# The last row of W_down in thirteen transfers of 16, 15, 14 … 5 and 2 partitions

## The chip, the cores and the metric

The kernel runs on one core of a Trainium2 chip. A core has TensorE (PE, with weight loads shown apart as PEld), VectorE (DVE), ScalarE (ACT), GpSimd (POOL) and SyncE (SP), and 16 DMA engines that move data between HBM and the core's SBUF memory. SBUF has 128 partitions. The metric is device time in microseconds, the median of several executions. One execution is recorded by the hardware profiler; it gives the page, the trace and all the views quoted here.

## The reference

Two layers follow each other for four sequences of one token each (B = 4, D = 576). The first is attention over a window of the last 4096 positions of a cache; the second is a gated MLP with F = 4608:

```
W = min(4096, max(256, Sk // 4))                    # 4096 of Sk = 16384
q = (layernorm(x) @ wq) -> [4, 32 heads, 1, 128]
scores = q . k * 128**-0.5 ; p = softmax(scores) ; o = p . v     # 16 kv heads
h = x + o.reshape(4, 1, 4096) @ wo

gate = layernorm(h) @ W_gate                        # [4, 4608]
up   = layernorm(h) @ W_up
hh   = gate * (gate > 0) * up
out  = h + hh @ W_down                              # W_down is [4608, 576]
```

All inputs are bfloat16. The cache windows and the weights that must be read are 159.6 MB.

## The kernel before

The program of each engine is written out by hand, in order. A small class `Sched` counts: an operation names what it depends on, and the class turns that into a wait on a semaphore value (`op`, `dma`, `wait`, lines 50 to 100). A transfer adds 16 to its semaphore when all of it has landed. Transfers that have the same key share a semaphore, so a wait on the last of several waits for the sum of all of them.

All large loads stand in one list, `transfers`, and SP issues them in that order (`prog_sync`, line 265). They go into one SBUF tensor, `pool`, which has four slots of 4 MB. A transfer waits until the reader of what stood there before is done (its `free` list). The order is: wq in two pieces (lines 234 and 236), then for 16 groups of four heads the K and V cache windows, alternating (lines 238 to 242), then wo (243), W_gate and W_up in two pieces each (245 to 249), and last W_down (251 to 256). The cache is the bulk of it: 32 transfers of 4 MB.

While the cache streams in, DVE transposes K (line 402), PE forms scores and the products with V (helper `mm`, lines 460 to 471), ACT takes the exponentials and POOL the maximum over partitions. After the last V, PE multiplies with wo (the `ATTN` step, lines 547 to 553), DVE adds the residual and normalises, PE forms gate and up, ACT and DVE combine them into `hhT`, and PE multiplies with W_down (lines 585 to 594).

W_down goes into SBUF with 36 of its rows on each partition: row p * 36 + j is at partition p, place j. A "row" of the transfer list means one place j on all 128 partitions, 576 values or 1152 bytes on each. The six transfers of before take 14, 9, 6, 4, 2 and 1 of these places, each over all 128 partitions. They wait for `ATTN`, because the space they fill was that of wo. PE waits for each transfer in turn and then adds its rows to the two output tiles, two matmuls a row (320 and 256 columns). When the last row is in, ACT and DVE copy one part each to `out_sb` (OUT0, line 367, and OUT1, line 454), and SP writes it out (line 268).

The x input is loaded by ACT's own queue at the start (line 303), over 4 partitions; the output is stored in the same shape.

Of the kernel before, what the change touches and what calls it, by code (L numbers as in the profile page):

```python
# [13 lines left out]
D = 576  # L14
# [24 lines left out]
JJ = 36  # L39
# [63 lines left out]
def bass_sequential_preLN__sliding_block_cached__glu_gated_reglu__decode_kernel(  # L103
# [12 lines left out]
    with ExitStack() as es:  # L116
        cnt = [0]

        def sb(name, shape, dt):
            return es.enter_context(nc.sbuf_tensor(name, shape, dt))  # L120

        pool = sb("pool", [128, NSLOT * QUAD], BF16)
# [77 lines left out]
        transfers = []  # L200
# [49 lines left out]

        wd_sb = pool[:, 0:FC * D].rearrange("p (j n) -> p j n", j=JJ)
        WD = [(0, 14), (14, 23), (23, 29), (29, 33), (33, 35), (35, 36)]
        for k, (f0, f1) in enumerate(WD):
            transfers.append((("wd", k), f"wd{k}", ["ATTN"],
                              lambda e, f0=f0, f1=f1: e.dma_start(
                                  out=pool[:, f0 * D:f1 * D], in_=B_W_down.rearrange("(p j) n -> p (j n)", j=JJ)[:, f0 * D:f1 * D])))

        def feat(c):
            return slice(c, c + 509, 4) if c < 4 else slice(512, D)
# [1 line left out]
        def land(name):  # L261
            return ("L",) + (name if isinstance(name, tuple) else (name,))
# [194 lines left out]
        def prog_pe(S):  # L457
# [126 lines left out]

            for k, (f0, f1) in enumerate(WD):
                deps = [land(("wd", k))]
# [44 lines left out]
```

## Time and profile before

| | |
|---|---|
| median of 3 runs | 377.74 us (377.72 to 378.39) |
| the profiled execution | 378.37 us |
| its span in the trace | 377.0 us |
| granted TensorE clock, mean | 0.923 |
| PE busy | 291.9 us (77%) |
| DVE busy | 222.5 us (59%) |
| HBM read | 159.58 MB, 423 GB/s over the span |
| transfers of W_down issued by SP | 353.51 to 356.21 us |

The span is the time from the first to the last instruction in the trace; the time of an execution has a little more around it. In the views, `out<-in` names the tiles an instruction writes and reads, "SPq" is SP's issuing of transfers, and the number after L is the line in the kernel. The busy share of DMA is a mean over the 16 engines. Below the page, the trace keeps one record for each DMA packet (its queue, start, duration and size, but not the engine that moved it) and the time of each semaphore update of a transfer.

### The profile page before, as it was taken

How to read it: one execution, taken by the hardware profiler on the slowest of the kernel's cores; microseconds unless marked ns; L12 is line 12 of the kernel's file. 1: busy time of each engine (PE TensorE's matmuls, PEld its weight loads, DVE VectorE, ACT ScalarE, POOL GpSimd, SP SyncE). 2: the span in 40 equal slices, each digit the busy share in tenths (PEclk: the TensorE clock that was granted, in tenths of full speed). 3: DMA queues.
4: the chain of work that ended last, by engine and by line, in shares of the span. 5: the costliest groups of instructions: out<-in, count | busy, mean ns of one | idle time of the engine just before them, and what ended most of it. 6: DMA issues, size and time to landing. Idle time of an engine off the chain costs nothing.

```text
span 377.0 us, 2565 instructions
## 1 busy us (share of the span) xinstructions
PE 291.9 (77%) x1384; PEld 67.9 (18%) x740; DVE 222.5 (59%) x169; ACT 53.1 (14%) x138; POOL 12.1 (3%) x34
## 2 busy tenths in 40 slices
PE   1408299969996999499939996799689967977675
PEld 0001012212221222022202221122112211222213
DVE  3037577696859494859476856775676658221230
ACT  3003402010220012001200220021002010101020
POOL 6000000000000000000000000000000000000000
PEclk9999879998998799989998998999869995996989
DMA  8999999999999999999999999999999999999995
GB/s 334 431 445 441 403 438 440 441 418 424 437 441 428 414 441 436 435 410 441 441 426 421 435 445 428 431 422 441 431 435 415 441 435 428 447 428 416 418 417 245
DMA packets 6507, 159.74 MB, mean 424 GB/s; under 512 B 729, under 2 KB 865, under 8 KB 1633
## 3 DMA queue, kind: packets, MB, share of 16 engines
q1 hardware_dynamic: 6488, 159.59, 98.7%
q8 instruction: 8, 0.13, 0.1%
q14 instruction: 3, 0.02, 0.0%
q10 hardware_dynamic: 8, 0.00, 0.0%
HBM read 159.58 MB, written 0.00 MB: 423 GB/s over the span
## 4 chain that ended last, share of the span: by engine, by line
DMA 53%; DVE 28%; PE 15%; ACT 2%; issue 1%; SPq 1%; POOL 0%; DVEq 0%
DMA pool<-in_A_k_cache_dram 48%; DVE kT L402 19%; PE sc L464 5%; PE sc L466 5%; DMA pool<-in_B_W_down_dram 5%; DVE acc L421 4%; DVE own_sb L418 2%; PE val L464 2%; PE val L466 2%; DVE probT L415 1%; DVE rmx L405 1%; ACT P L347 1%; DVE o_bf L440 0%; ACT L347 0%; ACT qz L336 0%
## 5 line engine op out<-in xcount | busy, mean ns | idle before, releaser
L402 DVE STREAM_TRANSPOSE kT<-pool 128x2048 f32<-128x2048 f32 x64 | 142.9, 2279 | 34.9 <-DMA pool<-in_A_k_cache_dram 33.9
L464 PE MATMUL sc<-kT,qz 128*128 128x512 bf16 x240 | 104.4, 435 | 28.7 <-DVE kT L402 28.7
L466 PE MATMUL sc<-kT,qz 128*128 128x512 bf16 x256 | 110.4, 431 | 18.3 <-DVE kT L402 16.2
L464 PE MATMUL val<-pool,probT 128*64 128x512 bf16 (+2 forms) x328 | 102.4, 360 | 4.6 <-DMA pool<-in_B_W_down_dram 4.6
L466 PE MATMUL val<-pool,probT 128*64 128x512 bf16 x256 | 96.2, 379 | 0.0
L464 PEld LDWEIGHTS sc<-kT,qz 128*128 128x128 bf16 x256 | 26.9, 105 | 154.8 <-issue 76.3
L464 PEld LDWEIGHTS val<-pool,probT 128*64 128x64 bf16 (+1 forms) x328 | 31.4, 104 | 88.0 <-issue 78.1
L405 DVE TENSOR_REDUCE rmx<-sc 128x1 f32<-128x1024 f32 x16 | 19.6, 1225 | 42.4 <-PE sc L466 42.4
L342 ACT ACTIVATE pmax<-mask,rmx 128x8 f32<-128x8 f32 x16 | 4.8, 301 | 241.3 <-DVE rmx L405 241.3
L415 DVE STREAM_TRANSPOSE probT<-P 128x1024 bf16<-128x1024 bf16 x16 | 19.9, 1245 | 20.7 <-ACT P L347 20.7
L347 ACT ACTIVATE P<-sc,bias 128x1024 bf16<-128x1024 f32 x16 | 17.8, 1113 | 13.3 <-DVE bias L410 13.3
L336 ACT COPY qz<-qrep 32x128 bf16<-32x128 bf16 x64 | 18.8, 294 | 0.6
L294 POOL PARTITION_ALL_REDUCE bcm<-pmax x16 | 5.9, 367 | 312.8 <-ACT pmax L342 312.8
L421 DVE TENSOR_REDUCE acc<-own_sb 128x128 f32<-128x1024 f32 x8 | 15.2, 1895 | 0.3
L418 DVE TENSOR_TENSOR own_sb<-val,mask 128x1024 f32<-128x1024 f32 x8 | 9.5, 1193 | 8.3 <-PE val L466 8.3
L464 PE MATMUL sc<-pool,oX 128*4 128x288 bf16 x32 | 10.2, 345 | 0.4 <-ACT oX L356 0.4
L408 DVE SCALAR_TENSOR_TENSOR t<-bcm,mask 128x8 f32<-128x8 f32 x16 | 2.7, 167 | 13.3 <-POOL bcm L294 13.3
L466 PE MATMUL sc<-pool,oX 128*4 128x288 bf16 x32 | 10.2, 343 | 0.0
L464 PE MATMUL sc<-qT,sel 32*128 32x128 bf16 x4 | 0.3, 284 | 9.8 <-DVE qT L428 9.8
L443 DVE TENSOR_TENSOR h_row<-sc,x_bf 4x576 f32<-4x576 f32 x1 | 0.7, 745 | 11.9 <-PE sc L466 11.9
L464 PE MATMUL sc<-col,foe 4*128 4x512 bf16 x16 | 6.4, 399 | 0.7 <-ACT qrep L322 0.7
L464 PE MATMUL val<-pool,xnT 128*32 128x512 bf16 x16 | 2.6, 628 | 5.0 <-DMA pool<-in_A_wq_dram 5.0
(98 smaller groups left out, 74.4 us busy)
## 6 DMA issues: line engine op xcount, KB each, us to landing
pool<-in_A_k_cache_dram SPq DMA_DIRECT2D x16, 4096.0 KB, 26.9
pool<-in_A_v_cache_dram SPq DMA_DIRECT2D x16, 4096.0 KB, 26.8
pool<-in_A_wo_dram SPq DMA_DIRECT2D x1, 4608.0 KB, 18.3
pool<-in_B_W_gate_dram SPq DMA_DIRECT2D x1, 4608.0 KB, 17.8
pool<-in_B_W_up_dram SPq DMA_DIRECT2D x1, 4608.0 KB, 24.0
pool<-in_A_wq_dram SPq DMA_DIRECT2D x1, 4096.0 KB, 13.6
pool<-in_B_W_down_dram SPq DMA_DIRECT2D x1, 2016.0 KB, 13.7
pool<-in_B_W_down_dram SPq DMA_DIRECT2D x1, 1296.0 KB, 16.4
```

The source lines that it names most:

```text
L294: S.op(g, lambda e, i=i: e.partition_all_reduce(bcm[:, i % 2, :], pmax[:, i % 2, :], 128, bass_isa.ReduceOp.max), deps=deps, name=("PAR", i))
L336: S.op(a, lambda e, src=src, dst=dst: e.copy(out=dst, in_=src), deps=deps, name=("QZ", i) if g == 3 else None, signal=g == 3)
L342: S.op(a, lambda e, i=i: e.activation(out=pmax[:, i % 2, :], in_=mask[:, 1, :], func=ACT.Identity, bias=rmx[:, i % 2:i % 2 + 1], scale=1.0 ...
L347: S.op(a, lambda e, i=i: e.activation(out=Pb[:, (i % 2) * 1024:(i % 2 + 1) * 1024], in_=sc[:, (i % 2) * 1024:(i % 2 + 1) * 1024], func=ACT ...
L402: S.op(v, lambda e: e.transpose(out=dst, in_=src), deps=deps, name=("TR", f))
L405: S.op(v, lambda e: e.tensor_reduce(out=rmx[:, i % 2:i % 2 + 1], in_=sc[:, (i % 2) * 1024:(i % 2 + 1) * 1024], axis=AX.X, op=ALU.max), dep ...
L408: S.op(v, lambda e: e.scalar_tensor_tensor(out=t8[:, :], in0=bcm[:, i % 2, :], scalar=-SCALE, in1=mask[:, 0, :], op0=ALU.mult, op1=ALU.mul ...
L415: S.op(v, lambda e: e.transpose(out=pT[i % NPT], in_=Pb[:, (i % 2) * 1024:(i % 2 + 1) * 1024]), deps=[("EXP", i)] + ([("PV", i - NPT)] if ...
L418: S.op(v, lambda e: e.tensor_tensor(out=own_sb[:, :].rearrange("p (x d) -> p x d", d=DH), in0=val[:, :].rearrange("p (x d) -> p x d", d=DH ...
L421: S.op(v, lambda e: e.tensor_reduce(out=acc[:, w % 2, :], in_=own_sb[:, :].rearrange("p (x d) -> p d x", d=DH), axis=AX.X, op=ALU.add), de ...
L464: return e.matmul(o, lhsT=l, rhs=r, start=start, stop=stop, skip_group_check=skip)
L466: return e.add_instruction(mybir.InstMatmult(name=nc.get_next_instruction_name(), start_tensor_calc=start, stop_tensor_calc=stop, bass_ski ...
```

## The change

The transfer of the last place of W_down (place 35, 147,456 bytes) becomes thirteen transfers. The first takes partitions 0 to 15, the second the next 15, then 14, and so on down to 5, and the last takes the remaining 2: 16 + 15 + … + 5 + 2 = 128. They share the semaphore of the piece, and PE waits for the sum of all thirteen. The first five transfers of W_down stay as they were.

```diff
         WD = [(0, 14), (14, 23), (23, 29), (29, 33), (33, 35), (35, 36)]
+        SHARES = (16, 15, 14, 13, 12, 11, 10, 9, 8, 7, 6, 5, 2)
         for k, (f0, f1) in enumerate(WD):
-            transfers.append((("wd", k), f"wd{k}", ["ATTN"],
-                              lambda e, f0=f0, f1=f1: e.dma_start(
-                                  out=pool[:, f0 * D:f1 * D], in_=B_W_down.rearrange("(p j) n -> p (j n)", j=JJ)[:, f0 * D:f1 * D])))
+            p0 = 0
+            for n in SHARES if k == len(WD) - 1 else (128,):
+                transfers.append((("wd", k) if p0 + n == 128 else ("wd", k, p0), f"wd{k}", ["ATTN"],
+                                  lambda e, f0=f0, f1=f1, p0=p0, n=n: e.dma_start(
+                                      out=pool[p0:p0 + n, f0 * D:f1 * D],
+                                      in_=B_W_down.rearrange("(p j) n -> p (j n)", j=JJ)[p0:p0 + n, f0 * D:f1 * D])))
+                p0 += n
```

The lines below it move down by five. No engine's list of instructions changes except SP's, which has twelve more transfers between the fifth one of W_down and the output.

## The prediction

> **What bounds the kernel now.** I read three views, from the whole to the end of the run: the page's DMA rows, the chain of work that ended last, and the busy shares of the last microseconds. The page first:
>
> ```profile
> DMA  8999999999999999999999999999999999999995
> DMA packets 6507, 159.74 MB, mean 424 GB/s; under 512 B 729, under 2 KB 865, under 8 KB 1633
> q10 hardware_dynamic: 8, 0.00, 0.0%
> HBM read 159.58 MB, written 0.00 MB: 423 GB/s over the span
> ```
>
> The 16 DMA engines are busy in every slice but the last, so the kernel is as long as its bytes plus what follows the last of them. The change moves no byte count; only the tail can move. The chain and SP's own timeline show the tail (start us, length us, what):
>
> ```profile
> 354.83 18.93 DMA pool<-in_B_W_down_dram
> 373.80 0.70 PE val L464 x7
> 374.51 0.68 PE val L464 x5
> 375.22 0.42 DVE out_sb L454
> ...
> 353.51 2.70 SPq L255 DMA_DIRECT2D pool<-in_B_W_down_dram  x6
> 375.71 0.35 SPq L268 DMA_DIRECT2D out_dram<-out_sb  x1
> ```
>
> SP issues the six transfers of W_down in 2.70 us and is then free until the output. TensorE waits for each piece in turn. The DMA view gives the landing of the last two (KB, us from issue to landing):
>
> ```profile
> pool<-in_B_W_down_dram SPq DMA_DIRECT2D x1, 288.0 KB, 19.2
> pool<-in_B_W_down_dram SPq DMA_DIRECT2D x1, 144.0 KB, 19.1
> ```
>
> Issued at 355.30 and 355.78 us (the 0.475 us steps of that row), they land at 374.47 and 374.83. The piece the change touches lands 0.36 us after the one before it, and 2.17 us before the end of the span at 377.0. Its two matmul pairs start at 374.88; those of the piece before it would let them start at about 374.76 (starts at 374.51 and 374.63, one more step of 0.11 to 0.13). So **an earlier landing of the last piece is worth at most 0.12 us**, and a later one is paid in full. The last view is the busy share by windows (window, its length, PE, PEld, DVE, ACT, POOL, PE clock, DMA share, GB/s):
>
> ```profile
> 373.25:373.50 0.25, 0.15 (x2) 0.00 (x0) 0.00 (x0) 0.00 (x0) 0.00 (x0) 1.00 0.61 221
> 373.50:373.75 0.25, 0.00 (x0) 0.00 (x0) 0.00 (x0) 0.00 (x0) 0.00 (x0) 1.00 0.48 171
> 373.75:374.00 0.25, 0.20 (x4) 0.18 (x6) 0.00 (x0) 0.00 (x0) 0.00 (x0) 1.00 0.13 46
> 374.00:374.25 0.25, 0.25 (x8) 0.15 (x3) 0.00 (x0) 0.00 (x0) 0.00 (x0) 1.00 0.05 18
> 374.25:374.50 0.25, 0.25 (x4) 0.00 (x0) 0.00 (x0) 0.00 (x0) 0.00 (x0) 1.00 0.05 18
> 374.50:374.75 0.25, 0.24 (x5) 0.09 (x4) 0.00 (x0) 0.00 (x0) 0.00 (x0) 1.00 0.00 0
> ```
>
> A share of 0.05 is one engine of 16: from 374.0 to 374.45 a single engine works, and the landing waits for it. The 16 semaphore updates of the last transfer say the same: counted from the first, 0, 0.10, 0.11, 0.29, 0.93, 1.16, then nine from 1.49 to 1.79, and one at 2.38 us. Four engines are done over 2 us early.
>
> **Packet prices.** In the trace's packet records the late engine ends the piece before with a 4-byte semaphore packet at 374.061, starts its eight 1152-byte rows at 374.067 and every 47 ns after that, and its last semaphore packet at 374.443; this lands 0.39 us later. So a row is 47 ns, a semaphore packet 6 ns, and the piece 0.38 us per engine.
>
> **The change, part by part.**
> - *One transfer of 128 rows becomes thirteen of 16 to 2 rows.* The 4-row load of x used four engines: its queue, q10, carried 8 packets, four rows and four semaphores. If n rows always go to n engines, and always the same first n, the engines in order carry 13, 13, 12, 12, 12, 11, 10, 9, 8, 7, 6, 5, 4, 3, 2 and 1 rows where each had 8, each row with a semaphore packet of its own.
> - *SP.* Twelve more issues of 0.43 to 0.55 us (the six above, and 0.55 for x on ACT's queue) with 0.04 between them: 5.7 to 7.1 us, so SP ends at 362 to 363.3 instead of 356.2. No engine reaches these rows before 371.7 (the late one's 374.07 less 2.38), and SP's next work is at 375.7. Cover of 8 us or more: nothing. Nothing else is queued behind them but the output, and ACT, DVE, POOL and PE issue what they issued.
> - *TensorE's wait* becomes one on all thirteen; it is still one wait, and OUT0 and OUT1 stand behind it as before.
> - *Where is the late engine in the order?* I followed the packets engine by engine (the next one starts 3 ns before the recorded end of the last). By the order in which engines start their first packet of wq the late one is the eighth; the first four are those that served x. So I take 9 rows for it; 1 and 13 are the ends.
> - *What does a one-row transfer cost its engine?* Low end: 53 ns, row and semaphore as above. There the semaphore stands behind eight packets, not one. High end: 0.39 + 0.05 = 0.44 us, if a transfer waited for the landing of the one before it on its engine. Below nothing is excluded: the bytes stay. The only one-row transfers with data behind them are those of x: on its four engines the next packet, of wq, took 714 to 829 ns (mean 772), on the next four in order 544 to 600 (mean 558), 0.21 us more. That is at the start-up of the queues, so part of it may be something else; I take half, 0.11, and so **0.16 us a transfer**.
>
> The sum: the late engine starts the rows at 374.06, takes 9 x 0.16 = 1.44, and lands 0.39 later: 375.89 against 374.83, or 1.06 us late. An engine with 13 rows from the group at 1.6 us starts at about 373.3, takes 2.08 and lands at 375.8, just before it. All of the 1.06 us is on the path, since nothing else is awaited. Made against the profiled execution (span 377.04, 378.37 with what lies around it, 0.63 above the median of 377.74) the span becomes 378.1; the same 1.06 us on the median gives **378.8 us**, 0.28% slower. At 0.44 a transfer the group with 13 rows bounds it: 373.3 + 5.7 + 0.39 = 379.4, or 4.6 us late; I hold that unlikely, because the landings of the last three whole pieces follow each other by 0.71 and 0.36 us, which their packets alone fill.
>
> The Trainium skill, DMA: Bandwidth & Descriptors, "Rules for kernel authors", says to coalesce many small transfers into one, since under 64 KB most of the time is overhead; these are 18 KB and less. Its "Anatomy of one DMA" puts a fixed cost of about 2.0 us on each transfer; twelve of those in a row would be an estimate of 24 us more, which this trace speaks against: six transfers queued together land as little as 0.36 us apart. What the fixed cost does inside one engine's queue no run here shows yet.
>
> **Rivals.**
> - *Only the rows count* (not slower). A transfer costs 53 ns or little more. With 9 rows the late engine is 9 x 53 = 0.48 against 0.38, 0.10 us later: 377.8. If it has 1 row, the 0.12 us above is gained: 377.6; with 12 rows, 0.25 is lost. It decides as long as a transfer stays under 0.127 us (9 of them, 0.75 us late). For it: the 6 ns between semaphore and next row. Against it: the x row. 377.6 to 378.5.
> - *The queue takes only so many transfers.* Before, eight were under way at 355.8 us (two of W_up, six of W_down), with no stall; after, it could be twenty. If SP were held at eight, each further issue waits for a landing, the ninth small one for about 374.6, and four more issues (0.48 each) and 1.3 us to land (the output's, from 375.71 to 377.01) end at 377.8: 3.0 us late, 380.7. Held at twelve it is 1.2 us, at sixteen nothing. For it: one issue of W_up took 1.48 us instead of 0.43. Against: five transfers were under way then, fewer than later.
> - *The rows do not spread.* The trace has only counts of 128 and 4. If an odd count falls on one engine, and in general on as many as the largest power of two in it, the first engine carries 81 rows: 81 x 0.047 + 0.08 = 3.9 us, from 371.7 to 373.3, so the landing is 1.1 to 2.7 us late: 378.9 to 380.5. That would be the change not doing what it says. The same page, "Why a DMA increments its semaphore by 16 and not by 1", has the largest divisor up to 16, so n rows on n engines; by that this rival falls.
> - *An instruction fetch falls elsewhere.* Single 8 and 16 KB instruction packets held engines back by 0.6 to 1.5 us before; one less on the late engine would bring the last landing down to the group at 1.79, 0.6 us less, one more would add as much.
>
> **How the numbers follow.** Forecast 0.42, with its own range of 0.127 to 0.28 us a transfer: 378.5 to 379.9. Only the rows 0.36. Queue limit 0.09. No spread 0.08. Fetch or drift of the measurement 0.05. 0.2% is 0.76 us, about what a measurement of this kernel can tell from no change. Slower holds the forecast, the queue and the missing spread, 0.59; same holds the rows, 0.36; faster 0.05, since the landing can give only 0.12 us. The range runs from the low end of the second case, 377.6, to 380.4, and leaves out the queue held at eight and transfers of over 0.3 us.
>
> **What the profile after would show.** Right: thirteen short issues at the last rows of W_down, all done by 363.5; the last one landing at about 375.9; the two matmul pairs of the last row starting there, and the piece before still landing at 374.5; windows after 374.5 with a DMA share of 0.05 to 0.15. Rows spaced by 53 ns would give the second case; SP issues stretching to 374 the third; a share of 0.06 from 374 to over 376 with one engine busy without a gap the fourth. I am wrong if the one-row transfers pass at the speed of their bytes, or if the late engine is not eighth in order.

## The result and the profile after

The kernel after takes **380.25 us** (median of 6 runs, 379.81 to 380.38) against 377.89 us for the kernel before (6 runs): a ratio of 1.006, 95% interval 1.0047 to 1.0073, which is 1.8 to 2.8 us more. The forecast was 378.8, slower. The direction held; the loss is 2.36 us where 1.06 was forecast.

The page of the kernel after, its DMA rows:

```profile
DMA  8999999999999999999999999999999999999994
DMA packets 6618, 159.74 MB, mean 422 GB/s; under 512 B 840, under 2 KB 976, under 8 KB 1744
q1 hardware_dynamic: 6600, 159.59, 98.3%
```

The same bytes in 112 more packets on SP's queue (6600 against 6488). That is 128 semaphore packets where the one transfer had 16: every transfer ran on as many engines as it has rows, so the rows did spread.

Next SP's timeline, and TensorE's weight loads for W_down, first after, then before (start, length, what; in brackets the idle time ahead of it and what ended it):

```profile
350.82 8.78 SPq L258 DMA_DIRECT2D pool<-in_B_W_down_dram  x18
...
373.30 0.36 PEld L469 LDWEIGHTS val<-pool,probT 128*4 128x4 bf16 x8 [0.24 <-DMA pool<-in_B_W_down_dram]
374.11 0.09 PEld L469 LDWEIGHTS val<-pool,probT 128*4 128x4 bf16 x4 [0.46 <-DMA pool<-in_B_W_down_dram]
376.37 0.08 PEld L469 LDWEIGHTS val<-pool,probT 128*4 128x4 bf16 x2 [2.17 <-DMA pool<-in_B_W_down_dram]
```

```profile
373.80 0.36 PEld L464 LDWEIGHTS val<-pool,probT 128*4 128x4 bf16 x8 [0.74 <-DMA pool<-in_B_W_down_dram]
374.51 0.09 PEld L464 LDWEIGHTS val<-pool,probT 128*4 128x4 bf16 x4 [0.36 <-DMA pool<-in_B_W_down_dram]
374.88 0.08 PEld L464 LDWEIGHTS val<-pool,probT 128*4 128x4 bf16 x2 [0.27 <-DMA pool<-in_B_W_down_dram]
```

The last line of each is the last row. It starts 2.26 us after the piece ahead of it where it started 0.37 us after: 1.89 us more. That step, from the second to last load to the last, is the measure used below; it compares kernels without the drift of the 370 us ahead of it. SP is not the reason: all 18 transfers are issued by 359.6 us.

Where the 2.26 us go is in the busy shares by windows (window, its length, PE, PEld, DVE, ACT, POOL, PE clock, DMA share, GB/s):

```profile
373.50:374.00 0.50, 0.50 (x8) 0.15 (x3) 0.00 (x0) 0.00 (x0) 0.00 (x0) 1.00 0.22 62
374.00:374.25 0.25, 0.14 (x5) 0.09 (x4) 0.00 (x0) 0.00 (x0) 0.00 (x0) 1.00 0.00 0
374.25:374.50 0.25, 0.25 (x4) 0.00 (x0) 0.00 (x0) 0.00 (x0) 0.00 (x0) 1.00 0.00 0
374.50:375.00 0.50, 0.04 (x1) 0.00 (x0) 0.00 (x0) 0.00 (x0) 0.00 (x0) 1.00 0.00 0
375.00:375.50 0.50, 0.00 (x0) 0.00 (x0) 0.00 (x0) 0.00 (x0) 0.00 (x0) 1.00 0.00 0
375.50:376.00 0.50, 0.00 (x0) 0.00 (x0) 0.00 (x0) 0.00 (x0) 0.00 (x0) 1.00 0.00 0
```

By the packet records the DMA engines are done at 373.98 us, TensorE ends the piece ahead at about 374.5, and from there to 376.3 the trace shows nobody at work. In its packet records the one-row transfers pass an engine every 53 ns, row and semaphore, and the last semaphore packet starts about 2.35 us before the last update of the semaphore lands; before, that lag was 0.39 us. So the end of a packet's record is not the end of its work here. The question for the experiments was what that work is.

### The profile page after: what moved, and what is told of

It reads as the page before. It is cut to its first block, busy times and chain, and to the rows that moved or that the text cites. A ratio compares the mean times of both kernels' runs of the same rounds, so it can differ in the third digit from the quotient of the medians.

```text
span 378.5 us, 2577 instructions
## 1 busy us (share of the span) xinstructions
PE 292.1 (77%) x1384; PEld 68.6 (18%) x740; DVE 222.5 (59%) x169; ACT 53.0 (14%) x138; POOL 12.1 (3%) x34
## 4 chain that ended last, share of the span: by engine, by line
DMA 46%; DVE 31%; PE 16%; ACT 3%; SPq 2%; issue 1%; POOL 0%; DVEq 0%
DMA pool<-in_A_k_cache_dram 41%; DVE kT L407 20%; PE sc L469 6%; PE sc L471 6%; DMA pool<-in_B_W_down_dram 5%; DVE acc L426 4%; DVE own_sb L423 2%; SPq L258 2%; PE val L469 2%; PE val L471 2%; DVE probT L420 2%; DVE rmx L410 2%; ACT P L352 2%; ACT pmax L347 0%; POOL bcm L299 0%
## 5 line engine op out<-in xcount | busy, mean ns | idle before, releaser
L469 PE MATMUL val<-pool,probT 128*64 128x512 bf16 (+2 forms) x328 | 104.7, 380 | 5.5 <-DMA pool<-in_B_W_down_dram 5.4
L469 PEld LDWEIGHTS val<-pool,probT 128*64 128x64 bf16 (+1 forms) x328 | 32.5, 108 | 90.2 <-issue 78.1
L469 PE MATMUL sc<-pool,oX 128*4 128x288 bf16 x32 | 9.5, 327 | 0.4 <-ACT oX L361 0.4
L471 PE MATMUL sc<-pool,oX 128*4 128x288 bf16 x32 | 9.5, 326 | 0.0
```

Of the source, the lines that this page charges most:

```text
L469: return e.matmul(o, lhsT=l, rhs=r, start=start, stop=stop, skip_group_check=skip)
L471: return e.add_instruction(mybir.InstMatmult(name=nc.get_next_instruction_name(), start_tensor_calc=start, stop_tensor_calc=stop, bass_ski ...
```

## The experiments

All edits start from the kernel after, if nothing else is said; `...` marks what is left out of an edit. The step from the second to last to the last load of W_down is read from each profile as above. The kernel before had medians of 378.04 to 378.07 us beside these runs. Expectations call "updates" the increments of the semaphore.

### A semaphore for each transfer

128 updates go to one semaphore in 4.2 us, 33 ns each; that could be the limit, though many of them come only 13 ns apart. So each transfer gets its own, and TensorE waits for all thirteen.

```diff
-  ... f"wd{k}", ["ATTN"],
+  ... f"wd{k}" if p0 + n == 128 else f"wd{k}_{p0}", ["ATTN"],
...
-  deps = [land(("wd", k))]
+  deps = [land(("wd", k))] + ([land(("wd", k, sum(SHARES[:i]))) for i in range(len(SHARES) - 1)]
+                              if k == len(WD) - 1 else [])
```

> The same thirteen transfers, each with a semaphore of its own; TensorE waits for all thirteen. Theory A (in each DMA engine the semaphore updates of its transfers land one behind the other, about 0.2 us each, while its rows pass at 53 ns): nothing changes, 380.2 us. Rival B (the 128 updates of one semaphore are taken one at a time, some 30 ns each): the landing comes with the packets, 378.0 us.

Measured: 380.17 us, ratio 1.0057 (1.0042 to 1.0072), and a step of 2.17 us:

```profile
374.06 0.09 PEld L469 LDWEIGHTS val<-pool,probT 128*4 128x4 bf16 x4 [0.44 <-DMA pool<-in_B_W_down_dram]
376.23 0.11 PEld L469 LDWEIGHTS val<-pool,probT 128*4 128x4 bf16 x2 [2.08 <-DMA pool<-in_B_W_down_dram]
```

The single semaphore is not the limit. And now the landing of each transfer can be read apart. In the trace's semaphore records the transfers of 12, 11, 10, 9, 8, 7 and 6 rows have their last update at 374.82, 375.02, 375.21, 375.41, 375.60, 375.81 and 376.01 us: **0.19 to 0.21 us apart, whatever their size**. The transfers of 5 and of 2 rows, which were issued last, land earlier, at 375.89 and 375.68. So the slowest engine here carries the transfer of 6 rows but not that of 5. If n rows always go to the same first n engines, as the prediction took it, that is the sixth in order, with 11 rows, neither the engines with 13 nor the eighth.

### Eight transfers of 16, thirty-two of 4

The number of updates stays at 128; what changes is how many fall on one engine.

```diff
-  SHARES = (16, 15, 14, 13, 12, 11, 10, 9, 8, 7, 6, 5, 2)
+  SHARES = (16,) * 8        # one kernel
+  SHARES = (4,) * 32        # another
```

> Eight transfers of 16 partitions: again 128 semaphore updates, but 8 on every engine instead of 13 to 1. Theory A: the last landing is 7 updates of about 0.2 us behind the first one, 1.0 to 1.2 us later than before, 378.9 to 379.1 us. Rival B: the same 128 updates, 380.2 us. If only the rows counted, as in the second case of the prediction: 378.0 us.

> Thirty-two transfers of 4 partitions: again 128 updates, now 32 on each of four engines. Theory A: 31 updates of about 0.2 us behind the first, 6.2 us, less up to 2.4 us if the four are among the engines that come early: 381.5 to 384 us. Rival B: 128 updates, 380.2 us.

Measured: 379.57 us (ratio 1.0039, 1.0024 to 1.0054) and 384.22 us (1.0162, 1.0147 to 1.0178). The last load of each:

```profile
375.65 0.08 PEld L469 LDWEIGHTS val<-pool,probT 128*4 128x4 bf16 x2 [1.35 <-DMA pool<-in_B_W_down_dram]
```

```profile
380.81 0.08 PEld L469 LDWEIGHTS val<-pool,probT 128*4 128x4 bf16 x2 [5.88 <-DMA pool<-in_B_W_down_dram]
```

The steps are 1.44 us (from 374.21) and 5.97 us (from 374.84): 0.18 and 0.19 us for each of the 8 and 32 transfers of an engine. Eight were 0.5 us dearer in the median than expected; the interval reaches down to 0.9 us, so it does not speak against 0.19.

### The first piece in eight transfers

If it is the transfer that costs 0.19 us, it should cost nothing where a row takes longer than that.

```diff
-  for n in SHARES if k == len(WD) - 1 else (128,):
+  for n in SHARES if k == 0 else (128,):           # with SHARES = (16,) * 8
```

> The last row is one transfer again; the first piece of W_down (14 places, rows of 16,128 bytes) goes in eight transfers of 16 partitions. Theory A: each row takes its engine about 0.6 us, longer than the 0.2 us of an update, and more data follows, so nothing is added: 377.9 us. Rival C (each small transfer costs SP, the queue or the engine something wherever it stands): 7 more on each engine at about 0.2 us, 379.3 us.

Measured: **389.35 us** (ratio 1.0316), far from every theory. The windows of this run say what happened, against the same window before (the first line is the kernel before):

```profile
368.00:370.00 2.00, 1.34 (x19) 0.78 (x15) 0.00 (x0) 0.00 (x0) 0.00 (x0) 1.00 0.97 406
```

```profile
368.00:370.00 2.00, 0.00 (x0) 0.00 (x0) 0.18 (x1) 0.00 (x0) 0.00 (x0) 0.50 0.99 178
```

The engines are as busy as ever, at 178 GB/s instead of 406, and a row of 16,128 bytes takes 1.49 us (median of the packet records) instead of 0.61. That suggested theory P: the place in SBUF that is written matters, since 16 neighbouring partitions are few ways in. And P would explain the small rows as well: if four engines that write to four neighbours share one way, four rows of 1152 bytes take 4 x 0.047 = 0.19 us, the very price found above. The next runs were made to separate the two.

### The same counts, other partitions

The partitions of a transfer are set 4 apart. Counts, engines, rows and updates stay as they were. The edit is shown against the kernel before.

```diff
+        STEPS = [(16 * a + j, 4, 4) for a in range(8) for j in range(4)]      # 32 x 4: start, count, step
+        STEPS = [(64 * a + j, 16, 4) for a in range(2) for j in range(4)]     # 8 x 16, in the other two kernels
...
+            sets = STEPS if k == len(WD) - 1 else [(0, 128, 1)]               # k == 0 in the third kernel
+            for i, (c, n, st) in enumerate(sets):
...
+                                  lambda e, f0=f0, f1=f1, rows=slice(c, c + (n - 1) * st + 1, st): e.dma_start(
+                                      out=pool[rows, f0 * D:f1 * D],          # in_ likewise
```

> Thirty-two transfers of 4 partitions as in the run of before, but the four are 4 partitions apart (0, 4, 8, 12, then 1, 5, 9, 13 and so on) instead of side by side. The same four engines, 32 rows and 32 updates each, the same issues. Theory A (updates land one behind the other): as with neighbours, 384.2 us. Theory P (four neighbouring partitions share one way into SBUF, about one engine wide, so four engines that write to neighbours each get a quarter of it): the four rows no longer meet, 32 x 53 ns = 1.7 us instead of 0.38 us on engines that may come early: 377.9 to 379.3 us.

> Eight transfers of 16 partitions, 4 apart (0, 4, ... 60; 1, 5, ... 61; and so on, then from 64). Theory A: 8 updates on each engine as with neighbours, 379.6 us. Theory P: the 16 rows of a transfer now go to at least eight places instead of four, two engines at one place at most, about 0.1 us a row: 378.0 to 378.5 us.

> The first piece of W_down (rows of 16,128 bytes) in eight transfers of 16 partitions, 4 apart; the last row is one transfer. With neighbours it was 389.4 us and a row took 1.49 us instead of 0.61. Theory P: at most two engines meet, a row takes 0.6 to 1.2 us: 378 to 383 us. Rival Q (transfers with one row for each engine are slow, whichever partitions they write): 389 us. Theory A has no cost here, neither with neighbours nor without.

Measured for the last row: 384.04 us (1.0159) and 379.33 us (1.0033, 1.0020 to 1.0047), against 384.22 and 379.57 with neighbours. The steps are 6.22 us (from 373.88) and 1.50 us (from 374.77) against 5.97 and 1.44:

```profile
380.10 0.08 PEld L468 LDWEIGHTS val<-pool,probT 128*4 128x4 bf16 x2 [6.13 <-DMA pool<-in_B_W_down_dram]
```

```profile
376.27 0.08 PEld L468 LDWEIGHTS val<-pool,probT 128*4 128x4 bf16 x2 [1.38 <-DMA pool<-in_B_W_down_dram]
```

**Which partitions are written plays no part for the one-row transfers**, so P is not the cause of the loss. For the first piece it does play one: 384.20 us (1.0166) against 389.35, a row takes 1.18 us, and the same window moves 207 GB/s:

```profile
368.00:370.00 2.00, 0.00 (x0) 0.00 (x0) 0.00 (x0) 0.00 (x0) 0.00 (x0) 0.50 0.98 207
```

What is P's alone was measured by itself, with one transfer more and not seven: the first piece as two transfers of 64 partitions.

```diff
+  SHARES = (64,) * 2        # for k == 0
```

> The first piece of W_down (rows of 16,128 bytes) in two transfers of 64 partitions, the last row whole. Only one transfer more, so theory A adds nothing: 378.0 us. Theory P (partitions side by side, and those of one half of SBUF, share ways in that are as wide as one engine): each transfer writes one half, so two engines meet at each way, a row takes 1.2 us as in the run with eight transfers 4 apart, and 8 x 0.6 = 4.8 us are added: 382.9 us.

Measured: 384.38 us (1.0177, 1.0152 to 1.0202), as with eight transfers 4 apart, a row at 1.20 us. So it is the partitions and not the number of transfers. The loss is 6.3 us where 4.8 was expected from the rows; the rest I did not trace. The Trainium skill, SBUF — State Buffer, "Door 1: The DMA port swizzle", says that partitions 0 to 63 reach only 8 of 16 ports. The runs agree: half of SBUF at a time takes 185 to 235 GB/s in the windows from 364 to 370 us, where the whole takes 406 to 417 in the kernel before. The last of these windows:

```profile
368.00:370.00 2.00, 0.00 (x0) 0.00 (x0) 0.00 (x0) 0.00 (x0) 0.00 (x0) 0.50 1.18 235
```

### The small transfers first

If the updates alone were late, the engines' other work would not notice. The thirteen transfers are put ahead of the five other pieces of W_down.

```diff
+  transfers[-18:] = transfers[-13:] + transfers[-18:-13]
```

> The thirteen transfers of the last row stand ahead of the other five pieces of W_down instead of behind them; TensorE still takes the rows in their old order, so its last three rows follow the landing of the piece of 2 rows, some 0.2 us more. Theory A: the updates land behind while the rows of the other pieces pass, nothing else: 378.2 us. Theory P: the engines with 13 rows lose 13 x (0.17 - 0.05) = 1.6 us at the small rows, and the bytes behind them come as much later: 379.5 to 380 us.

Measured: 379.81 us, ratio 1.0043 (1.0026 to 1.0059), 1.7 us more. Theory A as it was written falls: the delay stays with the engine and with everything queued behind it. The trace shows it in two ways. A row of 16,128 bytes took at most 0.61 us in the kernel before; behind the small transfers 24 of the 128 took over 0.8 us, up to 1.13. And from the landing of W_up's last piece to that of W_down's first, both averaged over the 16 engines, there are 5.80 us where there were 4.82 (4.92 in the kernel after): 0.9 to 1.0 us for 8 small transfers an engine on average, some 0.12 us each, row included. (The landings also lie further apart, 3.9 us from the first engine to the last where it was 2.4, but 3.2 us of that stood there ahead of the small transfers.) P gave the right time here, but the runs above took P away; the 0.14 us by which 0.19 is above a row's own 0.05 comes to 1.5 to 1.8 us on 11 to 13 transfers, much the same sum. So the theory now reads: **a transfer holds its engine for 0.19 us** where one-row transfers follow each other, in a place that the packet records do not show until about a dozen rows are queued up. That large rows behind them lose some 0.12 and not 0.19 us in the mean suggests that part of the hold passes beside them. (With 32 neighbouring transfers on an engine the records do show it: one engine, followed by the times of its packets, passes thirteen rows every 53 ns and from the fifteenth on one every 187 ns, and the median of a row's recorded time goes from 51 to 181 ns.)

### Fewer transfers

The dose at the low end, with 8 rows on each engine in every case.

```diff
+  SHARES = (32,) * 4        # one kernel
+  SHARES = (64,) * 2        # another, for the last piece
```

> Four transfers of 32 partitions: 4 updates and still 8 rows on each engine. Theory A, as the runs have left it (a transfer holds its engine for 0.19 us; rows of up to that time pass beside it): 4 x 0.19 = 0.76 instead of 0.38 us, 0.38 us more than before, 378.4 us. Theory A2 (a transfer adds 0.14 us to its rows): 4 x (0.10 + 0.14) less the 0.38 and the 0.14 that the one transfer of before has as well, 0.44 us more, 378.5 us. If only counts of 16 partitions or fewer are slow: 378.0 us.

> Two transfers of 64 partitions: 2 updates and 8 rows on each engine. Theory A: 2 x 0.20 (four rows, longer than the 0.19) = 0.40 instead of 0.38 us, 378.1 us. Theory A2: 0.14 us more than before, 378.2 us. Between these the run may not tell; both say that it is within 0.2% of before.

Measured: 378.53 us (1.0015, 1.0006 to 1.0024) and 378.36 us (1.0007, 0.9999 to 1.0016). Four transfers, then two, the last two loads of each:

```profile
374.27 0.09 PEld L469 LDWEIGHTS val<-pool,probT 128*4 128x4 bf16 x4 [0.51 <-DMA pool<-in_B_W_down_dram]
375.04 0.08 PEld L469 LDWEIGHTS val<-pool,probT 128*4 128x4 bf16 x2 [0.67 <-DMA pool<-in_B_W_down_dram]
```

```profile
374.15 0.09 PEld L469 LDWEIGHTS val<-pool,probT 128*4 128x4 bf16 x4 [0.33 <-DMA pool<-in_B_W_down_dram]
374.49 0.08 PEld L469 LDWEIGHTS val<-pool,probT 128*4 128x4 bf16 x2 [0.25 <-DMA pool<-in_B_W_down_dram]
```

| transfers on an engine | 1 | 2 | 4 | 8 | 8, 4 apart | 11 to 13 | 32 | 32, 4 apart |
|---|---|---|---|---|---|---|---|---|
| step to the last load, us | 0.37 | 0.34 | 0.77 | 1.44 | 1.50 | 2.26 | 5.97 | 6.22 |
| transfers x 0.19 us | 0.19 | 0.38 | 0.76 | 1.52 | 1.52 | 2.09 to 2.47 | 6.08 | 6.08 |

One and two transfers cost what their 8 rows cost (8 x 0.047 = 0.38); from four on the step is close to 0.19 us a transfer. Two transfers show no added cost in the step, four rows (0.19 us) passing beside the 0.19; that favours theory A's "beside" over A2's "on top", by one profile each. The times themselves do not tell these two apart. What in the engine takes the 0.19 us, the confirmation of the row or the update itself, no run separates: every transfer has both. With eight transfers and fewer the rows on an engine are the same 8 in every column, so it is the transfers that count. None of the versions was faster than before.

## Why the prediction was half right

The mechanism was right: each one-row transfer costs its engine a fixed time, and the loss is paid at the tail. The size was too small: 380.25 us lies above the 378.5 to 379.9 that the forecast case itself allowed, and inside the whole range only because that runs on to 380.4 for the rivals.

- *Direction, and the only path.* Right: only the tail moved, the wait for the last piece is paid in full, SP's issues are hidden (done at 359.6, forecast 362 to 363.3), the piece before lands about when it did (the loads for it start at 374.11 against 374.51).
- *The rows spread,* n rows to n engines: right, by the 112 packets. The queue did not stall at eight or twelve transfers either: all 18 were issued while the first was still to land. One issue took 1.52 us, off the path.
- *The price of a one-row transfer* was taken as 0.16 us, half way to the hint from the load of x. It is 0.19: 16% too low, and on 9 transfers 0.27 us. That the half came so near is luck: no run ties the slow start behind the load of x to this price, and the whole of the hint would have given 0.26.
- *The late engine.* This is the step that failed most: "So I take 9 rows for it". The sum put a single late engine at the bound, by its place in one profile. In the run with thirteen semaphores the bound was the sixth engine, with 11 rows, and which engine comes late changes between runs: the profile after has no single late one (the last two of the piece ahead land 0.05 us apart, where before the last stood 0.58 us behind the others). With the 0.19 us, 9 transfers on the late engine would be 1.33 us more than before, 11 would be 1.71 (1.82 at the 0.20 us between that engine's landings) and 13 would be 2.09; measured are 1.89 in the profile and 2.36 (1.8 to 2.8) in the medians. The profiled executions are one of the slowest before and the fastest after, so the medians differ by more. The eighth place itself is not shown either: the packets carry no engine, and it rests on following them by their times.
- *Where it would show.* Wrong: I expected a DMA share of 0.05 to 0.15 while the rows pass slowly. The share is 0.00. The packets pass at the 53 ns of the rival "only the rows count", and that rival would have seemed right from the packets alone; the landing decides.
- *0.39 us, the lag from the last semaphore packet to its landing,* was used as a constant. It grew to 2.35 us. This is not a further cost: it is the price of the transfers, which the prediction looked for in the packets and which came behind them.
- *The page's fixed cost.* The Trainium skill, DMA: Bandwidth & Descriptors, "Anatomy of one DMA", has about 2.0 us for a transfer, mostly waiting for the confirmation of the write; it gives this for transfers that GpSimd issues, and these are issued by SP. Queued on one engine, the runs have 0.19 us for each, so the change cost 2.4 us in the medians and not 24.

The prediction's high end of 0.44 us a transfer was set aside because whole pieces follow each other by 0.36 us. The table of the experiments shows what was weak there: with 8 rows behind each update, a fixed 0.19 us is hidden, and such rows can say nothing on it.

## What to carry to other kernels

A transfer costs each DMA engine that it uses a fixed time (0.19 us here), hidden where its share of the bytes takes longer; so count transfers per engine, not per kernel, and give each engine at least some 4 rows of 1152 bytes of a transfer (an engine's 8 rows took 0.77 us as four transfers of two, and 0.34 to 0.37 us as two of four or one of eight). Read the end of a load from the landing (the start of who waits for it), not from the DMA share, which read 0.00 for two microseconds here while the data was still awaited. And cut a large load over columns, as the first five pieces of W_down are, rather than over partitions: half the partitions at a time moved at about half the rate here.

## What the runs showed of the hardware that was not expected

- Splitting a 2 MB load by partitions costs far more than the number of transfers does: 11.3 us with 16 neighbouring partitions at a time, 6.1 us with 16 partitions 4 apart, 6.3 us with two halves of 64.
- Packet records of small rows run ahead of the landing. The last recorded packet of the thirteen transfers was over while their updates still came in for 2.35 us.
- Issuing 16 partitions that lie 4 apart took SP 0.56 to 0.59 us each, 16 neighbours mostly 0.42 to 0.43, and 15 neighbours and fewer mostly 0.29 to 0.47. The distance is not the whole reason: issues of 64 neighbours took 0.51 and 0.60 us. These are the durations of the single issues in the trace.
